# Late attention scores of a banded attention plus MLP kernel: plain float32 on quarters of the queries in place of high and low parts

## The chip, the cores and the metric

The kernel runs on one core of one Trainium2 chip. The metric is the device time of one execution in microseconds, the median of several runs. The core's engines work side by side and meet at semaphores: TensorE (PE: matmuls; PEld: its weight loads), VectorE (DVE), ScalarE (ACT), GpSimd (POOL) and SyncE (SP, which here issues nearly all DMA transfers). TensorE's instructions, SyncE's and GpSimd's run in the order in which the program is written; ScalarE's and VectorE's are put in order by a scheduler when the program is built.

## The reference, cut to what matters

Attention over 4 batches, 8 heads, 768 positions, head size 64. A query sees the first 8 positions and the 96 positions up to itself, with a bias that falls linearly with the distance (another slope for each head). Its result, all heads side by side, goes through an MLP with two weight matrices.

```python
scores = scale * np.matmul(q, k.transpose(0, 1, 3, 2))
is_global = pos[None, :] < int(n_global)                    # 8
is_local = (rel >= 0) & (rel < int(n_local))                # 96, rel = query - key
dist = np.where(is_global & ~is_local, float(n_local), np.abs(rel))
scores = np.where(is_global | is_local, scores - slopes[:, None, None] * dist, -1e9)
a = np.exp(scores - scores.max(-1, keepdims=True))
a = a / (a.sum(-1, keepdims=True) + 1e-09)
x = np.matmul(a, v)                     # then (batch * position, 512)
h = x @ w_in                            # 512 -> 2048
g = h * np.clip(h + 3.0, 0.0, 6.0) / 6.0
out = g @ w_out                         # 2048 -> 512
```

## The kernel before, in words

The 3072 tokens are 8 blocks of 384 tokens, each of three tiles of 128 queries. A block's attention is done in 4 pairs of heads, so there are 32 pairs, numbered 0 to 31. Each pair comes as one packed array (`pair_loads`): keys of both heads (head 0 on partitions 0 to 63, head 1 on 64 to 127; for each tile 96 earlier keys, 8 global ones and the tile's own 128, so 232 columns), the queries, and the values in two layouts.

Every product of the MLP is done three times with float32r parts, high times high, high times low, low times high. `first` (L168) has 12 matmuls for each of the 16 slices of the inner dimension, into a bank `hp`; `gate` (ACT L179, DVE L180), `high` (POOL L186 or ACT L188) and `rest` (DVE L193) make the parts of the activation; `second` (L200) has 9 matmuls of 512 columns into three banks `acc`. There are 8 x 16 slices in all.

The program has four stages:
- Up to about 66 us: the early pairs 0 to 8 (`plain` is true). Their scores (L857) are plain float32 matmuls of 64 rows; their exponentials are turned on TensorE (L904, L906, copied out by L908, `pt`). Beside it the weights are decoded from doubles (`decode`: L376, L388, L410 to L427).
- To about 158 us: the MLP of blocks 0 and 1, each slice as soon as its weights are decoded.
- To about 203 us (`rest_of_third`): the rest of block 1's MLP with pairs 9 to 11.
- Then the layers, blocks 2 to 7 (`twos`): one block's MLP with the next block's four pairs between its steps (`attention`). The last block has no attention beside it.

In the two last stages lists called `units` say what is written after which step of the MLP. In the layers a cycle of four units is: two `first` in a row, units 0 and 1, two `second` in a row, units 2 and 3. A pair takes six units: scores of a tile in each of the units 0, 1, 2; sums and norms of two tiles in 3; the third norm and the first `spread` in 4; the others and `fetch` in 5. Every second pair has the values of both pairs behind it, six units after its `fetch`.

A late pair, 9 to 31, has these steps:
- `split`: for each head ACT makes `q1`, the scaled query rounded to float32r (L831), POOL copies the keys to `kx` (L832), DVE makes the rest `q2` (L835) and the rest of the keys (L838). High and low part of a head's keys stand on the two halves of the partitions, and the queries come twice for that.
- `scores` (L861): for each tile and head two matmuls of 128 rows, 128 queries and 232 keys (128 in a block's first tile at a sequence's start). `bank` hands out one bank a tile, `sp` and `tp` in turn.
- `weigh`: DVE adds the distances and takes the minimum (L872), ACT makes the exponential and its sum (L876). `sum_up` (L886, L887) and `normalize` (POOL L896) divide by the sum.
- `spread`: DVE transposes blocks of 32 by 32 (L921), and a DMA writes them to DRAM (`there`, L923), one for each tile. `fetch` (L930): four DMAs bring them back turned, as `weights`.
- `values` (L948): 20 or 24 matmul instructions in 64 columns each, the two heads side by side.

## Time and profile before

| | |
|---|---|
| median of 3 runs | 660.93 us (660.62 to 661.12) |
| the profiled execution's own time | 660.32 us |
| its span, first to last instruction | 658.5 us |
| granted TensorE clock | 1.000 |
| late scores, L861 | 276 matmuls |
| fetches and writes of the exponentials | 92 and 69 DMAs |

A row of the profile reads: line, engine, operation, what is written <- what is read (shapes as partitions x elements), count | busy us, mean ns of one | idle time of the engine just before them, and what ended it. A row of the view in order of time begins with the start and the length in us, both from the span's start; equal neighbours are one row with a count, and the idle time before it stands in brackets with its releaser. Durations of neighbouring matmuls overlap, so the pace of TensorE is read from start to start. A plain float32 matmul of the code stands as two instructions in the trace.

### The profile page before, as it was taken

What the parts mean: (1) busy time and instruction counts of PE and PEld (TensorE: products, weight loads), DVE (VectorE), ACT (ScalarE), POOL (GpSimd) and SP (SyncE); (2) the same over time, 40 slices, a digit from 0 to 9 for tenths busy, and PEclk for the clock granted to TensorE, in tenths of its full rate; (3) what the DMA queues carried; (4) which work ended last, traced back from release to release, by engine and by line L of the source; (5) the groups of instructions that cost most, each with busy time, mean ns of one, the idle gap of its engine ahead of it and who ended that gap; (6) DMA issues with size and microseconds to landing.
All of it is one profiled execution on the core that took longest, in us unless ns stands there. A gap on an engine that the chain in (4) does not pass through costs nothing.

```text
span 658.5 us, 11444 instructions
## 1 busy us (share of the span) xinstructions
PE 647.1 (98%) x3933; PEld 581.0 (88%) x3933; DVE 423.2 (64%) x1147; ACT 286.4 (43%) x752; POOL 189.1 (29%) x377
## 2 busy tenths in 40 slices
PE   9989999999999999999999999999999999999997
PEld 7768899998989999999998999899899999989985
DVE  6888999998766876357654777356763676422222
ACT  6896877776333442244414333143331543121111
POOL 5663000002532433034241444124340342202100
PEclk9999999999999999999999999999999999999999
DMA  8676444432573675427552366615654275400001
GB/s 291 174 233 213 135 157 157 135 125 89 150 222 111 178 188 142 132 88 186 147 156 97 95 178 183 184 52 142 167 137 128 81 185 141 114 31 18 1 1 53
DMA packets 67316, 88.86 MB, mean 135 GB/s; under 512 B 10288, under 2 KB 52016, under 8 KB 67248
## 3 DMA queue, kind: packets, MB, share of 16 engines
q1 hardware_dynamic: 66960, 87.77, 45.9%
q8 instruction: 33, 0.54, 0.3%
q14 instruction: 35, 0.29, 0.1%
q10 hardware_dynamic: 288, 0.26, 0.1%
HBM read 65.08 MB, written 22.94 MB: 134 GB/s over the span
## 4 chain that ended last, share of the span: by engine, by line
PE 85%; DVE 9%; ACT 2%; issue 2%; POOL 1%; DMA 1%; POOLq 0%; DVEq 0%; ACTq 0%
PE hp L168 37%; PE acc L200 33%; PE xp L948 3%; PE sp L861 2%; PE tp L948 2%; PE tp L861 2%; PE sp L200 1%; DVE wz L423 1%; PE tp L200 1%; DVE wz L419 1%; PE xp L200 1%; DVE n L872 1%; ACT n L876 1%; DVE wz L411 1%; DVE g L180 1%
## 5 line engine op out<-in xcount | busy, mean ns | idle before, releaser
L179 ACT ACTIVATE g<-hp,small 128x384 f32<-128x384 f32 x127 | 73.6, 580 | 254.1 <-PE hp L168 147.2
L168 PE MATMUL hp<-xh,w1h 128*128 128x384 f32 x512 | 172.7, 337 | 0.4 <-ACT w1h L427 0.4
L168 PE MATMUL hp<-xh,w1l 128*128 128x384 f32 x512 | 172.3, 337 | 0.5 <-DVE w1l L416 0.5
L168 PE MATMUL hp<-xl,w1h 128*128 128x384 f32 x512 | 171.7, 335 | 0.0
L186 POOL TENSOR_SCALAR gh<-g 128x384 fp32r<-128x384 f32 x104 | 53.3, 512 | 289.1 <-DVE g L180 244.5
L180 DVE SCALAR_TENSOR_TENSOR g<-g,hp 128x384 f32<-128x384 f32 x128 | 70.2, 548 | 99.2 <-ACT g L179 98.8
L200 PE MATMUL acc<-w2h,gl 128*128 128x512 f32 x336 | 132.4, 394 | 0.2 <-DVE gl L193 0.2
L200 PE MATMUL acc<-w2h,gh 128*128 128x512 f32 x336 | 132.6, 395 | 0.0
L200 PE MATMUL acc<-w2l,gh 128*128 128x512 f32 x336 | 131.6, 392 | 0.0
L193 DVE TENSOR_TENSOR gl<-g,gh 128x384 fp32r<-128x384 f32 x128 | 75.9, 593 | 57.4 <-POOL gh L186 47.3
L896 POOL TENSOR_SCALAR n<-n,sums 128x232 f32<-128x232 f32 (+1 forms) x186 | 94.1, 522 | 48.4 <-DVE sums L887 42.5
L876 ACT ACTIVATE n<-n,least 128x232 f32<-128x232 f32 (+1 forms) x192 | 88.6, 464 | 30.4 <-DVE least L872 29.6
L168 PEld LDWEIGHTS hp<-xh,w1h 128*128 128x128 f32 x512 | 96.2, 188 | 3.4 <-ACT w1h L427 0.9
L168 PEld LDWEIGHTS hp<-xl,w1h 128*128 128x128 f32 x512 | 96.2, 188 | 2.1
L168 PEld LDWEIGHTS hp<-xh,w1l 128*128 128x128 f32 x512 | 96.0, 188 | 1.0 <-DVE w1l L416 0.8
L200 PEld LDWEIGHTS acc<-w2h,gl 128*128 128x128 f32 x336 | 63.0, 188 | 15.2 <-DVE gl L193 1.7
L200 PEld LDWEIGHTS acc<-w2h,gh 128*128 128x128 f32 x336 | 63.2, 188 | 13.3 <-issue 1.2
L200 PEld LDWEIGHTS acc<-w2l,gh 128*128 128x128 f32 x336 | 63.2, 188 | 11.6
L921 DVE STREAM_TRANSPOSE blocks<-n 128x256 f32<-128x256 f32 x127 | 49.4, 424 | 25.1 <-POOL n L896 23.1
L832 POOL TENSOR_SCALAR kx<-load 64x504 fp32r<-64x504 f32 (+1 forms) x46 | 29.1, 632 | 117.8 <-PE hp L168 96.1
L876 ACT ACTIVATION_READ_ACCUMULATOR n<-n,least 128x1 f32 x192 | 36.2, 188 | 0.0
L838 DVE TENSOR_TENSOR kx<-load,kx 64x504 fp32r<-64x504 f32 (+1 forms) x46 | 32.9, 715 | 1.8 <-POOL kx L832 0.4
(118 smaller groups left out, 731.5 us busy)
## 6 DMA issues: line engine op xcount, KB each, us to landing
wst<-w SPq DMA_DIRECT2D x32, 512.0 KB, 3.5
there<-blocks SPq DMA_DIRECT2D x58, 256.0 KB, 2.6
load<-pairs SPq DMA_DIRECT2D x23, 636.0 KB, 5.2
load<-pairs SPq DMA_DIRECT2D x32, 384.0 KB, 4.6
weights<-there SPq DMA_DIRECT2D x48, 192.0 KB, 3.6
weights<-there SPq DMA_DIRECT2D x44, 160.0 KB, 3.3
out<-o SPq DMA_DIRECT2D x23, 256.0 KB, 2.1
load<-pairs SPq DMA_DIRECT2D x8, 444.0 KB, 4.7
```

Of the source, the lines that this page charges most:

```text
L168: self.nc.tensor.matmul(hp, lhsT=self.w1(w, f)[:, kt, :], rhs=a[:, kt, :], start=(n == 0), stop=(n == 3 * NKT - 1))
L179: nc.scalar.activation(out=g, in_=hp, func=AF.Relu, bias=self.three, scale=1.0)
L180: nc.vector.scalar_tensor_tensor(out=g, in0=g, scalar=6.0, in1=hp, op0=ALU.min, op1=ALU.mult)
L186: self.nc.gpsimd.tensor_scalar(out=gh, in0=g, scalar1=1.0, scalar2=0.0, op0=ALU.mult, op1=ALU.add)
L193: self.nc.vector.tensor_tensor(out=gl, in0=g, in1=gh.bitcast(F32), op=ALU.subtract)
L200: self.nc.tensor.matmul(acc[tt], lhsT=a[:, tk], rhs=self.w2(w, f), start=(f == 0 and j == 0), stop=(f == NF - 1 and j == 2))
L832: nc.gpsimd.tensor_scalar(out=part["kx"][own, c], in0=k[own, c], scalar1=1.0, scalar2=0.0, op0=ALU.mult, op1=ALU.add)
L838: nc.vector.tensor_tensor(out=part["kx"][other, c], in0=k[own, c], in1=part["kx"][own, c].bitcast(F32), op=ALU.subtract)
L876: nc.scalar.activation(out=e[:, j, lo:W], in_=e[:, j, lo:W], func=AF.Exp, bias=self.least[:, i:i + 1], scale=-1.0, accum_out=self.sums[:, ...
L896: nc.gpsimd.tensor_scalar(out=e[:, j, lo:W], in0=e[:, j, lo:W], scalar1=over, scalar2=0.0, op0=ALU.mult, op1=ALU.add)
L921: nc.vector.transpose(out=blocks[:, :, s].rearrange("p b j q -> p j b q"), in_=e[:, :, c:c + P].rearrange("p j (b q) -> p j b q", b=4))
L948: nc.tensor.matmul(xps[j * D:(j + 1) * D, t * P:(t + 1) * P], lhsT=vt[0:K, t, j * D:(j + 1) * D], rhs=self.part(t, j, c, K), start=(c == 0 ...
```

## The change

For the late pairs the high and low parts go. The queries are scaled once a pair, in place, by ACT (`scale`, one operation of 128 x 384 with a scale for each partition from `over`), and the scores are plain float32 matmuls. A tile's 128 queries are split into four groups of 32. A group sees only 136 columns, its own window of 96 + 8 + 32 moved along by 32, in place of the tile's 232. Each of the 24 matmuls (3 tiles x 4 groups x 2 heads) uses a piece of the array of 64 rows by 32 columns. All are written together at the pair's first unit, head 0 into one bank, head 1 into another. Minimum, exponential and norm work on 136 columns.

A group's window begins 32 columns later than that of the group before. So in DRAM the blocks of group g go g places further, into a buffer whose unused places are set to zero once (`zeros_ahead`, 12 DMAs and a memset); two such buffers stay for good. The writes are four for each pair, one for each group, all behind the third tile's transposes; the fetches are eight. Every pair now fetches the whole of it. Masks for the groups (`packed_masks`) are made once by POOL, after the early pairs. The loads have the queries only once.

For one pair's scores on PE, pair 9 in the third block (`kx`, `q` are the parts, `load_72` is the loaded pair with its scaled queries; `acc` the banks of this stage), there stood:

```order
L861 MATMUL acc<-kx,q_1963 128x128
L861 MATMUL acc<-kx,q_1964 128x128
L861 MATMUL acc<-kx,q_1968 128x128
L861 MATMUL acc<-kx,q_1969 128x128
L861 MATMUL acc<-kx,q_1963 128x232
L861 MATMUL acc<-kx,q_1964 128x232
L861 MATMUL acc<-kx,q_1968 128x232
L861 MATMUL acc<-kx,q_1969 128x232
L861 MATMUL acc<-kx,q_1963 128x232
L861 MATMUL acc<-kx,q_1964 128x232
L861 MATMUL acc<-kx,q_1968 128x232
L861 MATMUL acc<-kx,q_1969 128x232
```

Now there stands, between the same neighbours (lines of the changed kernel: L206 is `second`, L174 `first`, L865 the packed scores):

```order
L206 MATMUL acc<-w2h_1028,gh 128x512
L206 MATMUL acc<-w2l_1029,gh 128x512
L206 MATMUL acc<-w2h_1028,gl 128x512
L865 MATMUL acc<-load_72 32x136 x24
L174 MATMUL hp<-xh,w1h_1026 128x384
L174 MATMUL hp<-xl,w1h_1026 128x384
```

The twelve are replaced by 24 smaller ones at the same place; in the layers the twelve stood in two groups, eight and four, on either side of a step of the MLP, and the 24 stand together.

On ACT, at the end of the early pairs (`pt` is a turned exponential on its way to the values, `wz` and `w1h` belong to the decoding, `gh` to the MLP), there stood:

```order
L908 COPY pt<-tp 128x2x128
L427 CAST w1h_143<-wz 128x4x128
L376 ACTIVATE wz<-wst 128x512
L188 CAST gh<-g 128x384
L908 COPY pt<-tp 128x512
L376 ACTIVATE wz<-wst 128x512
L154 CAST xh<-xp 128x384
```

Now:

```order
L930 COPY pt<-tp 128x2x128
L461 CAST w1h_143<-wz 128x4x128
L410 ACTIVATE wz<-wst 128x512
L194 CAST gh<-g 128x384
L851 ACTIVATE load_72<-load_72,over 128x384
L851 ACTIVATE load_73<-load_73,over 128x384
L930 COPY pt<-tp 128x512
L410 ACTIVATE wz<-wst 128x512
L160 CAST xh<-xp 128x384
```

The scalings of pairs 9 and 10 have moved ahead of the last copies of the early pairs; they wait for the pairs' loads and for `over`, which POOL writes. The old scalings of these pairs stood some 90 us later.

The diff, cut:

```diff
-QW = 2 * TB
+QW = TB
...
+GQ = 32
+GROUPS = P // GQ
+PW = PREV + NG + GQ
+SHIFT = GQ // 32
+AHEAD = 4 - SHIFT
+SPREAD = 4 + AHEAD
...
-                 "one": {"s": (o,), "x": (o,)}, "layers": {"s": (s, t), "t": (t,), "x": (x,)}}[self.stage][what]
+                 "one": {"s": (o,), "t": (o,), "x": (o,)}, "layers": {"s": (s,), "t": (t,), "x": (x,)}}[self.stage][what]
...
+    def packed_masks(self):
+        c, ts = self.const, self.nc.gpsimd.tensor_scalar
+        self.dl = c.tile([P, 2, PW], F32, name="dl")
+        self.over = c.tile([P, NPAIR], F32, name="over")
+        for h in range(H):
+            self.nc.gpsimd.memset(self.over[h % 2 * D:(h % 2 + 1) * D, h // 2:h // 2 + 1], float(-1.0 / (np.sqrt(D) * SLOPES[h])))
+        self.nc.gpsimd.memset(self.dl[:, 0], FAR)
+        for g in range(GROUPS):
+            rows, start = slice(g * GQ, (g + 1) * GQ), g * GQ
+            for out, d in ((self.dl[rows, 0, CB - start:], self.d0[rows, 0:start + GQ]),
+                           (self.dl[rows, 1], self.d1[rows, start:start + PW])):
+                ts(out=out, in0=d, scalar1=1.0, scalar2=0.0, op0=ALU.mult, op1=ALU.add)
...
-        for k in range(3):
-            pairs[0].split(k, False)
-        units[1] += [lambda: self.load_next(EARLY, False)]
+        pairs[0].scale()
...
-            at[0] += [lambda t=t, me=me: me.scores(t)() for t in range(NT)]
+            at[0] += [me.packed, lambda me=me: self.load_next(me.n, False)]
             at[1] += [me.sum_up] + [lambda t=t, me=me: me.normalize(t) for t in range(NT)]
-            at[2] += [lambda t=t, me=me: me.spread(t) for t in range(NT)] + [me.fetch]
-            for k in range(3):
-                at[k + 3 if last else k].append(lambda k=k, after=after: after.split(k))
+            at[2] += [lambda t=t, me=me: me.spread(t) for t in range(NT)] + [me.fetch, after.scale]
...
-            for t in range(NT):
-                at[t].append(lambda t=t, me=me: me.scores(t)())
-            if after:
-                at[3].append(lambda after=after: after.split(0))
+            at[0] += [me.packed, lambda me=me: self.load_next(me.n, False)]
             at[3] += [me.sum_up, lambda me=me: me.normalize(0), lambda me=me: me.normalize(1)]
             at[4] += [lambda me=me: me.normalize(2), lambda me=me: me.spread(0)]
             at[5] += [lambda me=me: me.spread(1), lambda me=me: me.spread(2), me.fetch]
-            for t in range(1, NT if after else 0):
-                at[t + 3].append(lambda t=t, after=after: after.split(t))
+            if after:
+                at[4].append(after.scale)
...
+    def scale(self):
+        nc, kk = self.nc, self.k
+        _, q, _, _ = kk.loaded(self.n)
+        nc.scalar.mul(out=q, in_=q, mul=kk.over[:, self.pr:self.pr + 1])
+
+    def packed(self):
+        nc, kk = self.nc, self.k
+        self.sums = kk.up.tile([P, 2, 2 * NT], F32, name="sums")
+        banks = [kk.bank(b)[:, 0:NT * PW].rearrange("p (t c) -> p t c", t=NT) for b in "st"]
+        keys, queries, _, _ = kk.loaded(self.n)
+        for t in range(NT):
+            for g in range(GROUPS):
+                own, c = slice(g * GQ, (g + 1) * GQ), t * TG + g * GQ
+                for j in range(2):
+                    rows = slice(j * D, (j + 1) * D)
+                    nc.tensor.matmul(banks[j][own, t], lhsT=queries[rows, t, own], rhs=keys[rows, c:c + PW], start=True, stop=True,
+                                     tile_position=(j * D, g * GQ))
+        for t in range(NT):
+            self.weigh(t, [bank[:, t] for bank in banks], kk.up.tile([P, 2, PW], F32, name="n"), 0)
...
-        nc.sync.dma_start(out=self.there[:, :, t, parts].rearrange("p b s c -> p b (s c)"),
-                          in_=blocks[:, :, parts].rearrange("p b s j q -> p b (s j q)"))
+        if t == NT - 1:
+            for g in range(GROUPS):
+                own = slice(g * GQ, (g + 1) * GQ)
+                nc.sync.dma_start(out=kk.there[self.n % 2][own, :, g * SHIFT:g * SHIFT + 4],
+                                  in_=self.blocks[own].rearrange("p s b t j q -> p s b (t j q)"))
...
-        for b in range(4):
-            self.nc.sync.dma_start(out=self.weights[32 * b:32 * b + 32].rearrange("p a t s j q -> p a (t s j q)")[:, :, part * 64:],
-                                   in_=self.there[:, b].rearrange("(a p) t s c -> p a (t s c)", a=4)[:, :, part * 64:])
+        for s in range(2):
+            for b in range(4):
+                rows = NG if s == 1 and b == 3 else 32
+                nc.sync.dma_start(out=to[32 * b:32 * b + rows, :, s],
+                                  in_=there[:, s, b + (0 if s else AHEAD)].rearrange("(a p) c -> p a c", a=4)[0:rows])
```

More of the change, by code (lines that the diff above doesn't have):

```diff
@@ L846, in scores @@
             self.sums = kk.up.tile([P, 2, 2 * NT], F32, name="sums")
-        if t != 1 or not self.plain:
-            self.banks = [kk.bank("s")[:, 0:2 * W].rearrange("p (i c) -> p i c", i=2) for _ in range(2 if self.plain else 1)]
-        sp = [self.banks[j][:, t % 2] if self.plain else self.banks[0][:, j] for j in range(2)]
+        if t != 1:
+            self.banks = [kk.bank("s")[:, 0:2 * W].rearrange("p (i c) -> p i c", i=2) for _ in range(2)]
+        sp = [self.banks[j][:, t % 2] for j in range(2)]
         e = kk.up.tile([P, 2, W], F32, name="n")
@@ L870, in weigh @@
             else:
-                d, scale = (kk.d0 if lo else kk.d1), SLOPES[h]
-            nc.vector.tensor_tensor_reduce(out=e[:, j, lo:W], in0=sp[j][:, lo:W], in1=d, op0=ALU.add, op1=ALU.min, scale=scale,
+                d, scale = kk.dl[:, 0 if self.first(t) else 1], SLOPES[h]
+            nc.vector.tensor_tensor_reduce(out=e[:, j, lo:end], in0=sp[j][:, lo:end], in1=d, op0=ALU.add, op1=ALU.min, scale=scale,
                                            scalar=3.0e38, accum_out=self.least[:, i:i + 1])
@@ L875, in weigh @@
             i = 2 * t + j
-            nc.scalar.activation(out=e[:, j, lo:W], in_=e[:, j, lo:W], func=AF.Exp, bias=self.least[:, i:i + 1], scale=-1.0,
+            nc.scalar.activation(out=e[:, j, lo:end], in_=e[:, j, lo:end], func=AF.Exp, bias=self.least[:, i:i + 1], scale=-1.0,
                                  accum_out=self.sums[:, 0, i:i + 1])
@@ L889, in normalize @@
     def normalize(self, t):
-        nc, e, lo = self.nc, self.rows[t], self.low(t)
+        nc, e, lo, end = self.nc, self.rows[t], self.low(t), self.end
         for j in range(2):
@@ L936, in part @@
             return self.pts[t][0:K, j, c, :]
[L937 removed]
+        return self.weights[0:K, :, c, t, j]
     def values(self, bank="x"):
@@ L943, in values @@
         for t in range(NT):
-            two = not self.low(t)
+            two = not self.first(t)
             for c in range(2 if two else 1):
```

92 lines of the change are left out of this document (37 added, 55 removed).

## The prediction

> **What bounds the kernel now.** I read the busy shares first, then the busy time by stretches, then the order in time around the steps that the change replaces. The head of the page:
>
> ```profile
> span 658.5 us, 11444 instructions
> PE 647.1 (98%) x3933; PEld 581.0 (88%) x3933; DVE 423.2 (64%) x1147; ACT 286.4 (43%) x752; POOL 189.1 (29%) x377
> ```
>
> The stretch from 238 us to the end of the layers, in the view by windows (columns: stretch, length, then busy us and instructions of PE, PEld, DVE, ACT, POOL, granted clock, DMA share, GB/s):
>
> ```profile
> 238.00:653.00 415.00, 415.00 (x2478) 377.04 (x2475) 224.92 (x601) 130.48 (x359) 120.06 (x236) 1.00 0.42 114
> ```
>
> PE has work in all 415.00 of 415 us, at the full clock. So what shortens PE's stream there shortens the kernel one for one, and what VectorE, ScalarE or GpSimd save brings nothing by itself. It matters only where PE waits for them. Before 152 us that happens: the decoding of the weights holds PE back at two places (used below).
>
> **The scores on PE.** The late pairs (9 to 31, 23 of them) use 12 matmuls each; all of them in one row of the windows view, and one pair in time:
>
> ```profile
> 150.00:653.00 503.00, 37.77 (x276) 37.08 (x276) 1.00 0.44 122
> 213.18 0.40 PE L200 MATMUL acc<-w2h,gl 128*128 128x512 f32 x1
> 213.41 0.60 PE L861 MATMUL tp<-kx,q 128*128 128x232 f32 x4
> 213.85 0.61 PE L861 MATMUL sp<-kx,q 128*128 128x232 f32 x4
> 214.30 0.34 PE L168 MATMUL hp<-xh,w1h 128*128 128x384 f32 x1
> ```
>
> 276 = 23 x 12. Durations overlap, so I count from start to start: 8 matmuls take 214.30 - 213.41 = 0.89 us, 0.111 each, and 12 take 1.33 us. Entering and leaving costs nothing visible.
>
> The new pair has 24 plain float32 matmuls of 64 rows by 32 columns on 136 keys: 8 places in the array, three rounds. The trace shows what plain float32 costs in the early scores, which run two halves of the rows at once, 232 keys wide:
>
> ```profile
> 25.06 0.46 PE L857 MATMUL sp<-load 64*128 64x232 f32 x1
> 25.07 0.46 PE L857 MATMUL acc<-load 64*128 64x232 f32 x1
> 25.36 0.36 PE L857 MATMUL sp<-load 64*128 64x232 f32 x1
> ...
> 25.56 0.36 PE L857 MATMUL sp<-load 64*128 64x232 f32 x1
> ```
>
> Each matmul of the code is two instructions here (one pair has 6 in the code, 12 in the trace), so the new pair has 48. Both halves start within 0.01 us, and the second instruction of one half doesn't hold up the first of the other. A step of both takes 25.56 - 25.36 = 0.20 us, 0.86 ns a key. If all eight places overlap as these two do, a step for 136 keys takes 0.117 us and a pair needs 3 x 2 = 6 steps, 0.70 us. The overhead of such a stay I take from the values, which also put two matmuls side by side:
>
> ```profile
> 314.57 0.34 PE L168 MATMUL hp<-xh,w1l 128*128 128x384 f32 x1
> 314.84 1.32 PE L948 MATMUL xp<-weights,load 128*64 128x128 f32 x20
> 315.99 1.27 PE L948 MATMUL tp<-weights,load 128*64 128x128 f32 x20
> 317.19 0.50 PE L200 MATMUL acc<-w2h,gh 128*128 128x512 f32 x1
> 317.52 0.40 PE L200 MATMUL acc<-w2l,gh 128*128 128x512 f32 x1
> ```
>
> From 314.57 to 317.52 are 2.95 us. Two ordinary steps (0.17 and 0.23) and 20 steps of 128 x 0.86 ns (2.20) leave 0.35 us for changing into and out of the split array. Eight starts in turn, up to 0.01 us apart, add some 0.05. So a pair takes 0.70 + 0.35 + 0.05 = 1.10 us against 1.33: -0.23 us, x 23 = **-5.3 us**. Bounds: 1.00 us (the turns hidden and the overhead a little less; -7.6) and 1.25 us (0.15 more, if PE's queue is refilled late; -1.8). 1.10 is nearest to the rows.
>
> Here a page speaks against the change. The Trainium skill ("TensorE: Matmul & The Clock Gate", section "Wait — 56ns, not 53.3ns?") says that matmul starts never come closer than about 25 ns, however few columns they have. By it 48 instructions would take 1.20 us, as an estimate from that page, and a pair 1.55 with the overhead: +5.1 us for 23 pairs in place of -5.3. The rows above show two starts 0.01 us apart, but on average no stay is denser than the values' 1.15 us for 20, so no row here settles it. By rows alone the case stands among the rivals.
>
> **One wait goes.** Pair 12 has its third query tile wait for a bank:
>
> ```profile
> 204.54 0.71 PE L861 MATMUL sp<-kx,q 128*128 128x232 f32 x4 [0.38 <-DVE least L872]
> ```
>
> PE is idle for 0.38 us. Now all three tiles of a head share one bank, so nothing in a pair waits for a bank: **-0.4 us**. No other wait of that kind stands on PE after 213 us.
>
> **Two scalings are early, on ScalarE.** `scale` for pairs 9 and 10 now stands among the last early pairs, ahead of a copy that PE waits for. The old scaling, and that place:
>
> ```profile
> L831 ACT ACTIVATE q<-load 128x384 fp32r<-128x384 f32 x46 | 21.5, 517 | 25.2 <-issue 9.2 <-PE sp L861 6.4 <-PE acc L861 5.1
> 57.99 0.58 ACT L908 COPY pt<-tp 128x512 f32<-128x512 f32 x1
> 58.72 0.30 PE L904 MATMUL tp<-ident,n 128*128 128x128 f32 x1 [0.33 <-ACT pt L908]
> 149.86 0.44 PE L168 MATMUL hp<-xh,w1h 128*128 128x384 f32 x1 [0.44 <-ACT w1h L427]
> 150.95 0.44 PE L168 MATMUL hp<-xh,w1l 128*128 128x384 f32 x1 [0.47 <-DVE w1l L416]
> ```
>
> Two scalings of 0.5 us ahead of the copy move PE's step at 58.72 by 1.0 us. Queued behind them on ScalarE is also the decoding's next `wz`, so VectorE comes late too. At 149.86 and 150.95 PE waits 0.91 us for the decoding anyway; a late PE would simply wait less there, as far as the decoding isn't late as well. Between 0 and 2.0 us (if GpSimd's eight small memsets that the scalings wait for, and its masks beside VectorE, cost once more as much); I take **+0.8 us**. The masks have no row of their own; GpSimd has nothing else from 57 to 150 us.
>
> **The way of the weights becomes longer.** The exponentials go to DRAM and come back: three writes and four fetches a pair, now four writes, all behind the third tile's transposes, and eight fetches. The second pair of each two has little time. Pair 15 (norms, writes, fetches, use):
>
> ```profile
> 252.48 1.31 POOL L832 TENSOR_SCALAR kx<-load 64x400 fp32r<-64x400 f32 x2
> 253.89 3.14 POOL L896 TENSOR_SCALAR n<-n,sums 128x232 f32<-128x232 f32 x6
> 256.12 2.25 SPq L923 DMA_DIRECT2D there<-blocks  x3
> 261.91 1.92 SPq L930 DMA_DIRECT2D weights<-there  x4
> DMA to landing us min/median/max: 2.9/3.7/3.9
> 267.60 1.53 PE L948 MATMUL tp<-weights,load 128*64 128x128 f32 x24
> ```
>
> The last fetch is issued at about 263.5 and lands by 267.4, 0.2 us ahead of its use. Now: the copy of the keys is gone from ahead of the norms (-1.4 us, 253.89 - 252.48), and the norms are shorter. A row with two norms of 128 and two of 232 columns gives their length:
>
> ```profile
> 287.12 1.59 POOL L896 TENSOR_SCALAR n<-n,sums 128x128 f32<-128x128 f32 x4 [3.04 <-DVE sums L887]
> ```
>
> At about 0.36 each for 136 columns, six take 2.2 instead of 3.14 (-0.9). Three more writes behind the last transpose at the fetches' spacing of 0.48 us: +1.4. Four more fetches: +1.9. The last one moves half the bytes and lands perhaps 1.3 us sooner (2.6 instead of 3.9, as the writes of 256 KB):
>
> ```profile
> there<-blocks SPq DMA_DIRECT2D x58, 256.0 KB, 2.6
> ```
>
> The sum is -0.3: no wait, for 15 and for the like pairs with more room. Pair 11, in the third block, has no key copy ahead of its norms:
>
> ```profile
> 185.14 2.86 POOL L896 TENSOR_SCALAR n<-n,sums 128x128 f32<-128x128 f32 x6
> 192.23 1.76 SPq L930 DMA_DIRECT2D weights<-there x4
> DMA to landing us min/median/max: 2.7/3.2/3.7
> 197.60 1.32 PE L948 MATMUL acc<-weights,load 128*64 128x128 f32 x20
> ```
>
> It lands at about 197.3 (193.6 + 3.7). Norms -0.7, writes +1.4, fetches +1.9, landing -1.1: +1.5, less 0.3 of room: PE waits **+1.2 us** once; between 0 (short issues) and 2.3 (landing as now).
>
> At nothing I cost what VectorE (two q2, two kx, narrower minima), ScalarE and GpSimd save, and the smaller loads: PE's work covers all of it. The load of the next-but-one pair now waits on SyncE for the packed matmuls; behind it stand only writes that come some 8 us later, and the scaling that needs it comes a whole pair later.
>
> **Sum** against the profiled execution's 660.32 us (span 658.5): -5.3 - 0.4 + 0.8 + 1.2 = -3.7, 656.6. The runs' median lies 0.6 above that execution, so 657.2.
>
> **Rivals.**
> Fewer than eight places at once (15%). Reading four column groups, or starting so many matmuls, may not go at the pace of two; the trace never shows more than two side by side. The point of balance: the six steps may take 0.98 us (1.33 - 0.35) instead of 0.70, so with under six of eight at a time the pair is slower than before. Four at a time: 12 x 0.117 + 0.35 = 1.75 us, +9.7 us instead of -5.3: 672.2. Two at a time, as now: 24 steps, 3.16 us: 704.6. Against it: the two halves start 0.01 us apart and don't hold each other up. The 25 ns of the Trainium skill ("TensorE: Matmul & The Clock Gate") would give 667.6 by the same sum.
>
> The weights come late for all second pairs (9%). If the norms start no earlier (the sums then decide) and a fetch lands as slowly as now, the second pair is 1.4 + 1.9 - 0.9 = 2.4 us later than before. Pair 15 has 0.2 us of room, and pair 25 has the most:
>
> ```profile
> 462.31 1.73 SPq L930 DMA_DIRECT2D weights<-there  x4
> weights<-there SPq DMA_DIRECT2D x44, 160.0 KB, 3.3
> 470.71 1.27 PE L948 MATMUL tp<-weights,load 128*64 128x128 f32 x20
> ```
>
> (The last fetch is issued at 463.6 and lands by 466.9 to 467.2, some 3.5 us ahead.) With the ten second pairs of the layers spread between 0.2 and 3.5, those under 2.4, some seven, wait 1.1 on average, 7 us in all, and pair 11 waits 1 us more: 665.2.
>
> The packed pair takes as long as the old one (10%): overhead of 0.55 us with eight places. Then 4.4 of the 5.3 are gone: 661.6.
>
> **Chances.** The forecast has 66%; its own range, with the bounds above but not all of them at once on one side, is 653 to 661.5. The third rival lies inside 662.5, the second around 665; a range of 653 to 664.5 leaves out the first, half of the second and a little at the low end, 20%. About 0.2% (1.3 us, so 659.6 to 662.3 for the median now) is what a measurement can tell from no change. Faster: 0.60 of the forecast's 0.66 and 0.01 of the third rival, 0.61. Same: 0.06 + 0.08 + 0.02 (forecast, third, second), 0.16. Slower: 0.15 + 0.07 + 0.01 (first, second, third), 0.23.
>
> **What would show it.** Right: from the last layer matmul to the first one after a packed stay about 1.1 us beyond an ordinary step, with eight starts close together; PE still without gaps after 240 us; no wait ahead of the third tile at pair 12; PE's step near 58.7 about a microsecond later; a gap of about 1 us ahead of pair 11's values near 197. Wrong: steps well over 0.117 us in the packed stay, or values of the second pairs with gaps ahead of them.

## The result and the profile after

The changed kernel takes 677.02 us (median of 4 runs, 675.32 to 682.26) against 660.79 us before: 1.0258 times as long (95% interval 1.020 to 1.0317), where 657.2 was forecast, with 653.0 to 664.5 as its range. The profiled execution took 675.99 us, 15.7 more than the one of before.

The head of the page, with the row of the granted clock in 40 slices, then the stretch from 238 us to the end of the layers (columns as before: busy us and instructions of PE, PEld, DVE, ACT, POOL, clock, DMA share, GB/s):

```profile
span 674.2 us, 13085 instructions
PE 648.5 (96%) x4761; PEld 570.2 (85%) x4761; DVE 356.3 (53%) x1066; ACT 267.3 (40%) x729; POOL 153.8 (23%) x349
...
PEclk9999999999998998999999999899999999999999
```

```profile
238.00:668.00 430.00, 420.02 (x3121) 372.27 (x3120) 178.66 (x555) 118.46 (x353) 91.46 (x205) 0.99 0.39 108
```

Two things are new: PE stands idle for 10 of these 430 us, and the clock isn't full in all slices. The engines that were to be relieved are (VectorE is busy for 356 us, in place of 423), and that brings nothing, as forecast.

One packed stay, its last layer step before and the first ones behind:

```profile
303.04 0.39 PE L206 MATMUL acc<-w2h,gl 128*128 128x512 f32 x1
303.36 0.30 PE L865 MATMUL sp<-load 64*32 64x136 f32 x1
...
303.41 0.30 PE L865 MATMUL tp<-load 64*32 64x136 f32 x1
303.50 0.28 PE L865 MATMUL sp<-load 64*32 64x136 f32 x1
...
303.62 0.28 PE L865 MATMUL sp<-load 64*32 64x136 f32 x1
...
304.05 0.28 PE L865 MATMUL tp<-load 64*32 64x136 f32 x1
304.25 0.45 PE L174 MATMUL hp<-xh,w1h 128*128 128x384 f32 x1
304.54 0.34 PE L174 MATMUL hp<-xl,w1h 128*128 128x384 f32 x1
```

Eight starts lie within 0.05 us (303.36 to 303.41), and the next eight follow 0.14 and then 0.12 us later. From 303.04 to 304.54 are 1.50 us; less two ordinary steps (0.23 and 0.17) the stay costs 1.10 us, the number of the forecast; 18 of the 23 stays, read in this way, take 1.10. So the loss lies elsewhere. What PE waited for:

```profile
PE sp L865 <- DVE xl L161: 4.3, 3, 3.3
PE acc L974 <- DMA weights<-there: 3.5, 2, 2.6
PE sp L974 <- DMA weights<-there: 3.3, 5, 1.3
...
PE hp L174 <- DVE g L186: 2.3, 1, 2.3
```

(us in total, times, longest.) The wait of 3.3 us for `xl`, ahead of pair 15's scores, is the longest. Followed back over the engines, two rows each of SyncE, ScalarE and PE in the view in order of time:

```profile
237.35 3.53 SPq L956 DMA_DIRECT2D weights<-there  x8
240.99 3.63 SPq L327 DMA_DIRECT2D load<-pairs  x3
245.01 0.62 ACT L851 ACTIVATE load<-load,over 128x384 f32<-128x384 f32 x1 [5.13 <-DMA load<-pairs]
248.53 0.47 ACT L160 CAST xh<-xp 128x384 fp32r<-128x384 f32 x1
248.17 0.39 PE L206 MATMUL acc<-w2h,gl 128*128 128x512 f32 x1
251.91 0.43 PE L865 MATMUL sp<-load 64*32 64x136 f32 x1 [3.35 <-DVE xl L161]
```

ScalarE sits for 5.13 us in front of a scaling (L851) whose load has only been issued at 240.99 us, behind the fetches of pair 13. It is the scaling of pair 16, whose scores come at 290 us. Behind it on ScalarE stand the gates of the layers and the halves `xh` of pair 12's and 13's output; `xl` needs `xh`, the bank of pair 13's values needs `xl`, and the packed matmuls of pair 15 need that bank. (That the chain runs over these steps is read from the order in time and from what each step waited for; the first experiment tests its cause.) All scalings of the kernel in one view:

```profile
L851 ACT ACTIVATE load<-load,over x23: 601/616/620, 58.6 to 553.0; 128x384 f32<-128x384 f32 x23
its engine sat idle before it (us, times) until:
  DMA load<-pairs: 88.8, 19
```

19 of 23 wait for their load, 88.8 us in all; the row of the old scalings, in the prediction, names no load among the causes of their 25.2 us. And behind a long stall PE runs slowly:

```profile
250.00:254.00 4.00, 2.10 (x50) 1.69 (x51) 2.07 (x7) 0.05 (x1) 0.60 (x2) 0.66 0.33 73
254.00:258.00 4.00, 4.00 (x14) 4.00 (x13) 1.37 (x12) 2.71 (x13) 0.00 (x0) 0.50 0.53 138
258.00:262.00 4.00, 4.00 (x21) 3.61 (x21) 1.11 (x2) 0.28 (x1) 0.52 (x1) 0.99 0.73 190
```

The granted clock (third column from the right) is 0.50 for some 7 us; 14 instructions in 4 us stand in the second row where the third has 21. The trace has three such stretches before the last layer matmul: 200.1 to 206.9, 251.3 to 258.1 and 425.4 to 428.8 us.

Where the 15.7 us went can be read by setting the start of each layer matmul beside that of the same matmul before (both kernels have the same 2688, in the same order; the figure is how far the changed kernel lies behind):

| up to (time of before) | what lies there | change, us |
|---|---|---|
| 157.8 | early pairs, decoding | 0.0 |
| 192.6 | packed stays of pairs 9 to 11 | -0.7 |
| 201.2 | pair 11's values late (4.5), half clock behind them (1.9) | +6.4 |
| 232.7 | pairs 12 to 14, the wait at pair 12 gone | -1.4 |
| 247.5 | pair 15's scores late (4.2), half clock behind them (2.2) | +6.4 |
| 269.1 | pair 15's values late | +1.5 |
| 387.4 | pairs 16 to 22 | -1.6 |
| 413.3 | pair 23's scores and a gate late (3.0), half clock behind them (1.6) | +4.6 |
| 423.8 | pair 23's values late | +2.0 |
| 559.0 | pairs 24 to 31 | -1.7 |

Before rounding the changes add up to 15.6 us. The clock is in two of the other figures too: the half clock began within pair 11's values and ahead of pair 15's scores. From the first packed matmul of pair 15 to the next layer matmul are 1.54 us, where the stay at 303.36 has 0.89; the second half of pair 11's values took 1.48 us from its start to the next layer matmul, where all of them took 1.24 before.

### The profile page after: what moved, and what is told of

It reads as the page before. It is cut to its first block, busy times and chain, and to the rows that moved or that the text cites. A ratio compares the mean times of both kernels' runs of the same rounds, so it can differ in the third digit from the quotient of the medians.

```text
span 674.2 us, 13085 instructions
## 1 busy us (share of the span) xinstructions
PE 648.5 (96%) x4761; PEld 570.2 (85%) x4761; DVE 356.3 (53%) x1066; ACT 267.3 (40%) x729; POOL 153.8 (23%) x349
## 4 chain that ended last, share of the span: by engine, by line
PE 63%; DMA 10%; DVE 8%; SPq 6%; ACT 5%; POOL 4%; issue 3%; POOLq 0%; ACTq 0%
PE hp L174 28%; PE acc L206 25%; DMA there<-blocks 4%; SPq L956 4%; DMA load<-pairs 3%; ACT n L898 2%; POOL n L918 2%; DVE blocks L940 2%; SPq L945 2%; PE xp L974 2%; ACT g L185 2%; DVE g L186 2%; DMA weights<-there 1%; PE sp L865 1%; PE sp L206 1%
## 5 line engine op out<-in xcount | busy, mean ns | idle before, releaser
L174 PE MATMUL hp<-xh,w1h 128*128 128x384 f32 x512 | 176.2, 344 | 2.3 <-DVE g L186 2.3
L174 PE MATMUL hp<-xh,w1l 128*128 128x384 f32 x512 | 174.2, 340 | 0.1
L174 PE MATMUL hp<-xl,w1h 128*128 128x384 f32 x512 | 173.6, 339 | 0.0
L206 PE MATMUL acc<-w2h,gh 128*128 128x512 f32 x336 | 133.5, 397 | 0.0
L206 PE MATMUL acc<-w2h,gl 128*128 128x512 f32 x336 | 132.1, 393 | 0.2 <-DVE gl L199 0.2
L206 PE MATMUL acc<-w2l,gh 128*128 128x512 f32 x336 | 131.9, 393 | 0.0
L199 DVE TENSOR_TENSOR gl<-g,gh 128x384 fp32r<-128x384 f32 x128 | 71.6, 559 | 66.2 <-POOL gh L192 57.4
L174 PEld LDWEIGHTS hp<-xh,w1h 128*128 128x128 f32 x512 | 97.6, 191 | 8.9 <-issue 3.5
L898 ACT ACTIVATE n<-n,least 128x136 f32<-128x136 f32 (+2 forms) x192 | 79.4, 415 | 55.3 <-DVE least L894 54.5
L174 PEld LDWEIGHTS hp<-xl,w1h 128*128 128x128 f32 x512 | 97.8, 191 | 2.6
L174 PEld LDWEIGHTS hp<-xh,w1l 128*128 128x128 f32 x512 | 97.6, 191 | 0.8 <-DVE w1l L450 0.7
L918 POOL TENSOR_SCALAR n<-n,sums 128x136 f32<-128x136 f32 (+2 forms) x186 | 82.2, 460 | 40.9 <-DVE sums L909 30.8
L206 PEld LDWEIGHTS acc<-w2h,gh 128*128 128x128 f32 x336 | 63.4, 189 | 15.3 <-issue 3.6
L206 PEld LDWEIGHTS acc<-w2h,gl 128*128 128x128 f32 x336 | 63.2, 188 | 14.4 <-DVE gl L199 0.9
L206 PEld LDWEIGHTS acc<-w2l,gh 128*128 128x128 f32 x336 | 63.3, 188 | 11.5
L940 DVE STREAM_TRANSPOSE blocks<-n 128x256 f32<-128x256 f32 x138 | 51.2, 424 | 23.0 <-POOL n L918 20.5
L851 ACT ACTIVATE load<-load,over 128x384 f32<-128x384 f32 x23 | 14.1, 615 | 88.8 <-DMA load<-pairs 88.8
L865 PE MATMUL sp<-load 64*32 64x136 f32 x480 | 19.6, 289 | 4.3 <-DVE xl L161 4.3
```

What stands on the lines that cost most here:

```text
L174: self.nc.tensor.matmul(hp, lhsT=self.w1(w, f)[:, kt, :], rhs=a[:, kt, :], start=(n == 0), stop=(n == 3 * NKT - 1))
L199: self.nc.vector.tensor_tensor(out=gl, in0=g, in1=gh.bitcast(F32), op=ALU.subtract)
L206: self.nc.tensor.matmul(acc[tt], lhsT=a[:, tk], rhs=self.w2(w, f), start=(f == 0 and j == 0), stop=(f == NF - 1 and j == 2))
L851: nc.scalar.mul(out=q, in_=q, mul=kk.over[:, self.pr:self.pr + 1])
L865: nc.tensor.matmul(banks[j][own, t], lhsT=queries[rows, t, own], rhs=keys[rows, c:c + PW], start=True, stop=True, tile_position=(j * D, g ...
L898: nc.scalar.activation(out=e[:, j, lo:end], in_=e[:, j, lo:end], func=AF.Exp, bias=self.least[:, i:i + 1], scale=-1.0, accum_out=self.sums ...
```

## The experiments

Two theories stood after the trace. Theory 1: the scaling on ScalarE waits for its load and holds up the gates, the exponentials and the halves of x behind it. Theory 2: the way of the weights (turn, write, fetch) has become too long, because nothing is written until the last transposes are done.

**Scalings as written.** ScalarE's order is the scheduler's, while those of PE, SyncE and GpSimd are held to the written order. The edit holds the scalings of pairs 11 to 31 too:

```diff
+        before = [i.name for i in nc.cur_bb.bb.instructions if i.engine == mybir.EngineType.Activation and "Tile" not in type(i).__name__][-1]
         nc.scalar.mul(out=q, in_=q, mul=kk.over[:, self.pr:self.pr + 1])
+        if self.n > EARLY + 1: kk.tc.add_manual_dep(nc.cur_bb.bb.instructions[-1], before, mybir.DependencyInfo(
+            mybir.DependencyClass.NoSync, mybir.DependencyReason.DATA), reason="as written")
```

> The changed kernel, with one edit: ScalarE keeps the scalings of pairs 11 to 31 behind the instruction of ScalarE that is written last ahead of them, so that the scheduler can't draw them forward to a place where their load hasn't landed. Theory 1 (the scaling: ScalarE waits for the load, and the gates, exponentials and parts of x behind it come late): ScalarE's 88.8 us of waiting for loads go to under 10; the waits of PE ahead of pair 15's scores (3.35 us), at 409 and at 424 us go with the two drops of the granted clock behind them (5 us in all), pair 11's values wait about 1.6 us in place of 3.5 and so keep the full clock: 655 to 660 us. Theory 2 (the weights' way alone: four writes behind the last transposes): ScalarE waits for other things in place of the loads, the stalls stay, 673 to 679 us.

Measured: 660.61 us, 0.9998 times the kernel before (0.9988 to 1.0008), so 16.4 us less than the changed kernel, just above the range of theory 1. ScalarE waits for no load any more; the scaling of pair 16 now stands behind the gate and runs at once:

```profile
241.66 0.58 ACT L185 ACTIVATE g<-hp,small 128x384 f32<-128x384 f32 x1 [1.96 <-DVE gl L199]
242.14 0.60 ACT L851 ACTIVATE load<-load,over 128x384 f32<-128x384 f32 x1
242.68 0.48 ACT L160 CAST xh<-xp 128x384 fp32r<-128x384 f32 x1
```

No wait of PE is left between 210 and 650 us; the late values of pairs 15 and 23 went with the late scores. One part missed: pair 11's values wait as long as before.

```profile
PE acc L974 <- DMA weights<-there: 3.7, 2, 2.5
```

Its sums came 3.0 us sooner (182.0 in place of 185.0 us), its last weights only 0.3 us. So for 15 to 31 theory 1 holds, for 11 it doesn't.

**Two writes.** The four writes of 32 partitions become two of 128, to the same addresses (cut: the buffer gets a second view, `turned`, whose rows lie a group apart):

```diff
-            for g in range(GROUPS):
-                own = slice(g * GQ, (g + 1) * GQ)
-                nc.sync.dma_start(out=kk.there[self.n % 2][own, :, g * SHIFT:g * SHIFT + 4],
-                                  in_=self.blocks[own].rearrange("p s b t j q -> p s b (t j q)"))
+            for s in range(2):
+                k = s * SPREAD * NT * 64
+                nc.sync.dma_start(out=kk.turned[self.n % 2][:, :, k:k + 4 * NT * 64],
+                                  in_=self.blocks[:, s].rearrange("p b t j q -> p (b t j q)"))
```

> The changed kernel, with one edit: the exponentials of a pair go to DRAM in two writes of 128 partitions in place of four of 32 partitions, to the same addresses. Both theories: the last write is issued 1.3 us sooner, and fetches, loads and scalings follow by 1.0 to 1.9 us. Theory 2 (the weights' way): nearly all stalls are 0.1 to 2.7 us long, so most of them go: 659 to 664 us. Theory 1 (the scaling): the waits of ScalarE for loads grow shorter by as much, but stay (over 50 us of the 88.8), PE still waits ahead of pair 15's scores for 1.5 to 2.5 us: 666 to 671 us.

Measured: 822.56 us, 1.2457 times the kernel before; both theories missed by 150 us. SyncE's order shows where:

```profile
184.72 1.13 SPq L946 DMA_DIRECT2D there<-blocks  x2
197.01 3.54 SPq L957 DMA_DIRECT2D weights<-there  x8
```

The fetches wait for the writes until 197.01, 11.7 us behind the last issue. For the 23 pairs this time is 11.1 to 12.2 us; with four writes, in the changed kernel, it was 3.1 to 4.6 us. In the trace 16 completions belong to each write of four, and only 5 to each of these two. The first of the 5 comes 0.9 to 1.0 us behind the issue, the other four between 6.8 and 11.6 us behind it. The target of the new write has the four groups as its outermost dimension. The Trainium skill ("DMA: Bandwidth & Descriptors", section "Why a DMA increments its semaphore by 16 and not by 1") says that a transfer uses as many of the 16 engines as divide the slowest dimension of both sides, and that the engines not used are counted at once; by it these writes ran on four engines (four completions and one jump), and the trace agrees. The run says nothing on the theories.

**Both edits.**

> Both edits: the scalings of pairs 11 to 31 stay where they are written, and two writes in place of four. Theory 1 and theory 2 agree that no stall over 0.5 us is left on PE behind 160 us, and that the clock stays full: the packed pairs' saving shows whole, 23 x 0.25 = 5.8 us, so 654 to 656 us. A rival with a cause not seen so far (the packed matmuls themselves lower the clock): the drops stay, over 660 us.

Measured: 785.39 us (1.1894; 1.1855 to 1.1933). The two writes spoil this run too; that it lies 37 us below the run with them alone shows only that the scalings cost something there as well.

**The writes alone, in the kernel before.** Its own scores, scalings and fetches, but four late writes (and with them, as in the changed kernel, one buffer for the transposed blocks in place of three; the trace shows no wait for it):

```diff
-        self.bp = self.pool("bp", 3, side="right")
+        self.bp = self.pool("bp", 1, side="right")
...
-        blocks = kk.bp.tile([P, 4, 2, 2, 32], F32, name="blocks")
+            self.blocks = kk.bp.tile([P, 4, NT, 2, 2, 32], F32, name="blocks")
...
-        nc.sync.dma_start(out=self.there[:, :, t, parts].rearrange("p b s c -> p b (s c)"),
-                          in_=blocks[:, :, parts].rearrange("p b s j q -> p b (s j q)"))
+        for g in range(4 if t == NT - 1 else 0):
+            own, part = slice(g * 32, (g + 1) * 32), slice(64 if self.low(0) else 0, None)
+            nc.sync.dma_start(out=self.there[own].rearrange("p b t s c -> p b (t s c)")[:, :, part],
+                              in_=self.blocks[own].rearrange("p b t s j q -> p b (t s j q)")[:, :, part])
```

> The kernel before, with one edit: its exponentials go to DRAM as in the changed kernel, in four writes of 32 partitions behind the third tile's transposes, in place of one write behind each tile's; scores, loads and fetches are its own. Theory 2 (the writes make the way 3.4 us longer by themselves): with the room that the second pairs had (0.2 to 3.5 us) they wait 1.5 us on average, 17 us in all and more if the clock drops: 672 to 682 us. If the writes cost 1.5 us only, as the prediction's sum had it, five pairs wait 3.3 us in all: 663 to 665 us. Theory 1 alone (the stalls need the scaling): within 2 us of the kernel before.

Measured: 670.57 us (1.0137; 1.0109 to 1.0166), 9.9 us more than the kernel before. That is in none of the ranges: below the 672 to 682 of theory 2, above the 663 to 665 by the prediction's price of the writes, and far from theory 1 alone.

```profile
PE tp L950 <- DMA weights<-there: 3.8, 4, 1.4
PE acc L950 <- DMA weights<-there: 2.6, 1, 2.6
```

The values of second pairs now wait (L950 is the values' line). So late writes cost by themselves. With the scalings as written, the changed kernel has the same late writes, and only pair 11 waits for them. What pays the price back for the others is most likely that the copies of the keys are gone from ahead of the norms and that the norms are shorter (pair 11 had no such copies); no run separates these.

**Pair 11: another queue for its writes.** In the scalings-as-written kernel, SyncE around pair 11:

```profile
184.31 3.54 SPq L956 DMA_DIRECT2D weights<-there  x8
187.96 0.82 SPq L327 DMA_DIRECT2D load<-pairs  x2
188.87 3.55 SPq L945 DMA_DIRECT2D there<-blocks  x4
195.10 3.55 SPq L956 DMA_DIRECT2D weights<-there  x8
```

Pair 11's last transpose ended at 186.8, but its writes stand behind pair 10's fetches and two loads. Theory 3: that queue makes them late.

```diff
-                nc.sync.dma_start(out=kk.there[self.n % 2][own, :, g * SHIFT:g * SHIFT + 4],
+                (nc.gpsimd if self.n < 12 else nc.sync).dma_start(out=kk.there[self.n % 2][own, :, g * SHIFT:g * SHIFT + 4],
```

> The first experiment's kernel (scalings of pairs 11 to 31 as written), with one more edit: the writes of pairs 9, 10 and 11 are issued by GpSimd in place of SyncE. Theory 3 (SyncE's queue is the bound of the third block's pairs: a pair takes 1.9 us of write issues, 4.0 us until the last of them lands, 3.2 us of fetch issues and 0.4 to 0.9 us for loads, about 10 us, against 9.5 us from pair to pair, so that pair 11's writes are issued 2.0 us behind its transposes): the writes of pair 11 start within 0.5 us of its last transpose, its last fetch lands some 2 us sooner, near 196.5 us, its values wait under 1.2 us in place of 3.7, the clock stays full, and the span shortens by 4.5 to 6 us: 654.5 to 656 us. Rival (a write's own 4 us from issue to landing make pair 11 late, not the queue): its last fetch lands at most 0.5 us sooner, the stall and the drop of the clock stay: 659.5 to 661 us.

Measured: 661.31 us (0.9996; 0.998 to 1.0012). The writes did follow their transposes at once (188.3, then 188.6 us), yet they took up to 6.1 us to land (2.9 to 6.1, median 4.0), and the next fetches began later than before:

```profile
DMA to landing us min/median/max: 2.9/4.0/6.1
```

```profile
196.50 3.55 SPq L956 DMA_DIRECT2D weights<-there  x8
```

The loads, issued at 189.19 and 189.65 beside them, landed among them (194.2 and 195.9; the last write 196.4). The place in SyncE's queue alone wasn't it. The run is no clean test of it, though: GpSimd, which now issues writes between its other work, came later to its copies and norms, so that pair 11's transposes ended 1.5 us later (188.3 in place of 186.8), and PE waited 0.7 us for a copy at 173 us.

**All writes from GpSimd.** `nc.gpsimd` for all pairs.

> As the run before, but GpSimd issues the writes of all pairs. Theory 3: nothing more is gained in the layers, where no value waits any more; SyncE's queue gets shorter by 1.9 us a pair. If a write costs GpSimd as much as SyncE (0.63 us of issue each, and the wait for the transposes ahead of it, some 3.4 us a pair) the copies gh behind them come up to 1 us late at places, which PE does not see: 654.5 to 656.5 us. If GpSimd needs more than 1.5 us for one write, gh is late and PE waits: over 660 us.

Measured: 661.88 us (1.001; 0.9998 to 1.0021). GpSimd needs 0.5 us for a write, far less than the 1.5 us from which a loss was expected; still nothing is gained, and the values of one more pair wait (0.9 us near 502 us).

**Idle matmuls while PE waits.** Twelve matmuls ahead of pair 11's values, into the bank that they overwrite:

```diff
-        xps = kk.bank(bank)[:, 0:TB]
-        for t in range(NT):
+        xps, any_ = kk.bank(bank)[:, 0:TB], kk.three.broadcast_to([P, P])
+        for t in [None] * (12 * (self.n == 11)) + list(range(NT)):
+            if t is None: nc.tensor.matmul(xps[:, 0:P], lhsT=any_, rhs=any_, start=True, stop=True); continue
```

> The first experiment's kernel, with 12 idle matmuls of 128 columns (into the bank that the values then overwrite) ahead of pair 11's values, so that PE is busy while it waits for the weights. If the drop of the granted clock behind this stall (200.0 to 206.9 us, 1.95 us of the drift against the kernel before) comes from PE standing idle, the clock stays full and only the wait is left: 658.5 to 659 us. If it has another cause (the packed matmuls, the kernel's power), it stays: 660.6 us, or more by what the idle matmuls delay.

Measured: 659.63 us (0.9976; 0.9962 to 0.9989). The first two rows are the stretch around pair 11's values with the scalings as written alone, the last two the same stretch with idle matmuls (PE busy, clock, DMA share, GB/s):

```profile
200.00:204.00 4.00, 3.17 (x17) 0.51 0.94 300
204.00:208.00 4.00, 4.00 (x17) 0.64 0.26 88
```

```profile
200.00:204.00 4.00, 2.95 (x33) 1.00 0.80 192
204.00:208.00 4.00, 4.00 (x24) 1.00 0.81 311
```

The clock stays full with the weights as late, the same packed matmuls and the same data: it is the idle PE that lowers it. The time lies above the 658.5 to 659 us expected. In the profiled execution the clock dropped elsewhere, near 60 us, where PE waits for the early pairs' copies (0.82 between 58 and 62 us); the 12 runs lie between 658.2 and 661.7 us.

**All scalings as written**, those of pairs 9 and 10 too (the condition on `self.n` left out).

> The first experiment's kernel, with the scalings of pairs 9 and 10 left where they are written too, so that none stands among the early pairs. PE's step near 59 us should come 1.0 us sooner. Theory (the decoding of the weights covers it, as the 0 end of the prediction's term had it): the two waits for the decoding near 150 us take the 1.0 us back, and the time is within 0.5 us of the first experiment's 660.6. The prediction's middle value: 0.8 us less, 659.8 us.

Measured: 661.01 us (0.9994; 0.9984 to 1.0005), as the first experiment. PE's step near 59 us comes sooner (59.38 in place of 60.06), and the waits for the decoding near 150 us are back: the early scalings cost nothing on average, the 0 end of the term.

**Two loads out of the way.** The load of pair 11's values ahead of pair 10's fetches, that of pair 13's keys behind pair 11's:

```diff
-            at[0] += [me.packed, lambda me=me: self.load_next(me.n, False)]
+            at[0] += [me.packed]
...
-            at[2] += [lambda t=t, me=me: me.spread(t) for t in range(NT)] + [me.fetch, after.scale]
-        units[10].append(lambda: pairs[0].values("x"))
+            at[2] += [lambda t=t, me=me: me.spread(t) for t in range(NT)] + ([] if p == 1 else [me.fetch]) + [after.scale]
+            at[2 if p == 2 else 0].append(lambda me=me: self.load_next(me.n, False))
+        units[10] += [lambda: pairs[0].values("x"), pairs[1].fetch]
```

> The first experiment's kernel, with SyncE's order changed in the third block alone: the load of pair 11's values stands ahead of pair 10's fetches in place of behind them, and the load of pair 13's keys and queries behind pair 11's fetches in place of ahead of its writes. In the first experiment these two loads (187.96 and 188.41 us) were issued between pair 10's fetches and pair 11's writes, and the first of the writes landed only behind them (192.26). Theory 3 in its second form (what is queued ahead of pair 11's writes, on SyncE and at the DMA engines, makes them late): the writes are issued at about 187.6 and have landed by 192 in place of 195.0, the last fetch lands by 198 in place of 200.7, PE waits about 1.9 us in place of 3.7, and the clock stays full: 656.5 to 657.5 us. If a write needs its 4.2 us anyway: the last fetch lands at about 199.5, the clock drops as before: 659 to 660 us.

Measured: 658.22 us (0.9957; 0.9944 to 0.9971).

```profile
188.86 2.49 SPq L946 DMA_DIRECT2D there<-blocks  x4
194.11 3.53 SPq L957 DMA_DIRECT2D weights<-there  x8
```

The writes are issued as before (188.86), since pair 10's fetches began 0.9 us later, but they have landed 1.0 us sooner (194.11 in place of 195.10). PE waits 2.4 us in place of 3.7, and the low clock lasts half as long (3.41 us in place of 6.83). The time lies between the two ranges. So the second form of theory 3 holds in part. What is left is the way itself: 5.2 us from first write to first fetch, and 5.5 to the last weights, together more than the 9.5 us from pair to pair.

**The same with six idle matmuls.**

> As the run before, with 6 idle matmuls ahead of pair 11's values. If the wait there is short enough for the clock to stay full by itself, they bring nothing (656.5 to 657.5 us, as the run before); if the clock drops in the run before, they take the drop away and it is 1.5 to 2 us faster than that run.

Measured: 657.26 us (0.9942; 0.9928 to 0.9955); the intervals of this and the run before overlap. In its profile the clock is full around 200 us and again dropped near 60 us (0.95 between 58 and 62).

**A third room for the loads**, with the scheduler's scalings of the changed kernel:

```diff
-        return self.room[(n if n < EARLY else LAST[(n - EARLY) % ROOMS]) % MORE]
+        return self.room[n % MORE] if n < EARLY else self.late[(n - EARLY) % 3]
...
-            self.load(n + ROOMS, values)
+            self.load(n + 3, values)
```

> The changed kernel, with ScalarE's order left as it is there (the scalings drawn forward), but with three rooms for the loads of the late pairs in place of two, so that a load is issued a whole pair earlier. Theory 1 (the loads come too late for the place of the scalings): ScalarE's waits for loads go from 88.8 us to under 15, the waits of PE at pairs 15 and 23 go as in the first experiment, only pair 11's stay: 659 to 662 us. If the place of the scalings hurts in another way (their 0.6 us ahead of gates and exponentials): over 668 us.

Measured: 680.43 us (1.0309; 1.0288 to 1.033): a clear miss.

```profile
L855 ACT ACTIVATE load<-load,over x23: 598/616/624, 58.7 to 532.6; 128x384 f32<-128x384 f32 x23
...
  DMA load<-pairs: 85.2, 17
```

The loads come a pair earlier, and ScalarE still waits 85.2 us for them. From pair 15 on a scaling starts 16 to 46 us ahead of its pair's matmuls in the changed kernel, 37 to 60 us here, and 3 to 26 us where it stays as written. It seems that the scheduler moves the scaling forward as far as it takes the load to allow, so that more room moves the wait and doesn't end it; what the scheduler assumes of a load is in no run. The expectation had taken the order of ScalarE for unchanged. The scalings do stand at like places (245.01 us there and 246.70 us here, each ahead of a gate), but each is that of the next pair (17 in place of 16).

**All together**: every scaling as written, the loads aside, six idle matmuls.

> All scalings as written (those of pairs 9 and 10 too), SyncE's two loads aside in the third block, and 6 idle matmuls ahead of pair 11's values: the three edits that took something away, in one kernel. The profile of the run before this one (with the scalings of pairs 9 and 10 still early) had left the early pairs with PE 2.6 us behind the kernel before, 1.6 us of it by a drop of the clock near 60 us. If the early scalings bring that drop, it is gone here, and of the 23 x 0.25 = 5.8 us of the packed pairs and the 0.4 of pair 12 only the rest of pair 11's wait is lost, about 2 us: 656 to 657 us, ratio to the kernel before 0.993 to 0.995. If the drop near 60 us has another cause, it comes in some of the runs here too: a median of 657 to 658 us with a spread of 2 us.

Measured: 656.40 us, 0.993 times the kernel before (0.9916 to 0.9944), 4.9 us less.

```profile
span 654.5 us, 13114 instructions
PE 641.0 (98%) x4773; PEld 565.3 (86%) x4773; DVE 357.7 (55%) x1066; ACT 268.4 (41%) x729; POOL 153.5 (23%) x349
```

```profile
PE acc L976 <- DMA weights<-there: 1.0, 1, 1.0
```

That is within the 656 to 657 us expected. One wait of 1.0 us for weights is left, and the clock doesn't drop before the last layer matmul (its mean over the span is 0.999). A saving of the forecast's size (3.7 us) is there, but the change alone doesn't bring it: it needed three more edits, of which the forecast knew nothing.

## Why the prediction was wrong

**The packed stay (-5.3): right.** 1.10 us forecast, 1.10 measured, 0.12 us a step with all eight places at work. Where nothing waits, the comparison gives 0.27 us a pair in place of 0.23, so the old pairs took a little more than the 1.33 us counted. The first rival, fewer places at once, is out: 48 starts lie within 0.69 us (303.36 to 304.05), 15 ns apart on average. The 25 ns between starts that the Trainium skill gives ("TensorE: Matmul & The Clock Gate", section "Wait — 56ns, not 53.3ns?") is not a bound for matmuls in different places of the array: the trace disagrees.

**Pair 12's wait (-0.4): right.** About 0.6 us, the part of its step in the comparison (0.9) that is not the 0.27 us of its stay.

**The early scalings (+0.8): too much.** PE's step came 1.66 us late at that place,

```profile
60.38 0.30 PE L926 MATMUL tp<-ident,n 128*128 128x128 f32 x1 [1.58 <-ACT pt L930]
```

and by 157.8 us nothing of it was left: the waits at 149.86 and 150.95 took it in, as the lower end said. With all scalings held back the step was still 0.7 us late, so 1.0 us of the 1.66 belongs to the scalings, as forecast; what delays the rest no run separates. What the term lacked is that the longer wait sometimes lowers the clock there.

**What was costed at nothing: the step that failed.** The prediction said of the load of the next-but-one pair that behind it stand only writes that come 8 us later, "and the scaling that needs it comes a whole pair later". The second half failed: it took the place in the code for the place on the engine. The section on the change shows that two scalings stand some 90 us ahead of the old ones, and the prediction priced these two; it didn't ask where the other 21 stand. 19 of the 23 waited for their load, 88.8 us in all, with gates, exponentials and parts of x behind them. And the load's own place was overlooked: it is issued behind the fetches of the pair before, which wait for writes to land. Pair 14's packed matmuls ended at 232.9 us; the load that they set free was issued at 240.99. Holding the scalings back gave 16.4 us, more than the whole loss against the kernel before.

**Pair 11 (+1.2, at most 2.3): mis-sized, 6.4.** The rows of SyncE, two from before and two from after:

```profile
186.77 2.58 SPq L923 DMA_DIRECT2D there<-blocks  x3
192.23 1.76 SPq L930 DMA_DIRECT2D weights<-there  x4
189.84 3.48 SPq L945 DMA_DIRECT2D there<-blocks  x4
195.70 3.56 SPq L956 DMA_DIRECT2D weights<-there  x8
```

From the last transpose (189.8) to the first fetch are 5.9 us where 3.4 were before (188.8 to 192.23): +2.5 in place of the +1.4 for writes. The sum had priced the issues of three more writes; but all of a pair's data, too, now starts on its way behind the transposes. The fetches, +1.9 less 1.1, cost 0.2 (5.1 us before and 5.3 now from first issue to last landing): the later issues land sooner. The norms save 0.3, not 0.7 (2.57 us in place of 2.86: a norm takes the 0.36 us counted, but the first of the six 0.77). They began 1.3 us later, behind a wait of ScalarE of 4.97 us for a load ahead of the exponentials. That is 3.7; with the start due 0.7 us sooner by the packed stays, less 0.3 of room, 4.1 of the 4.5 us seen. PE stood idle for 3.5 of these (the row of the waits above); most of the rest is the half clock on the second half of the values. The other 1.9 us is the half clock behind them.

**The clock: in no term and no rival.** Behind the stalls half clock took 5.7 of the 15.7 us (1.9 + 2.2 + 1.6), and some more within pair 11's values and pair 15's scores. It always began in a stall that other causes made, or up to 1.2 us behind it.

**The second rival (weights late for all second pairs, 665.2)** came nearest to a part of what happened: in the kernel before the late writes alone cost 9.9 us. In the changed kernel with the scalings as written only pair 11 waits for its weights by more than 0.2 us, so all second pairs waiting is not what made the loss. The range failed because the place of the scalings had no price at either end.

## What to carry to other kernels

Where a scheduler orders an engine, a new instruction need not stand where it was written: look at that engine's order for every copy of it, and ask for each what it waits for and who stands behind it. A stall's price on PE is its length and the half clock behind it: here waits of 2.3 to 3.4 us cost another 1.6 to 2.9 us by the half clock, one of 1.3 us nothing more. Data that is written early, piece by piece, hides its own transfer behind the work on the next piece; gathered into one write behind the last piece, all of it is on the path.

## What the runs showed of the hardware

The clock drops on a grid: every low stretch in the 14 traces begins a whole number of 3.41 us behind the first entry of the clock's record, and lasts a whole number of them too, if the record doesn't end first: one or two in most traces, up to five (17.07 us) in the two runs with two writes. The Trainium skill ("TensorE: Matmul & The Clock Gate", section "What's actually happening") gives that window, and one idle window as the condition. The length agrees; the condition doesn't, if idle means all of it: the drop at 425.4 us followed an idle stretch of only 2.3 us,

```profile
424.21 0.44 PE L174 MATMUL hp<-xh,w1h 128*128 128x384 f32 x1 [2.32 <-DVE g L186]
```

in a window (421.96 to 425.37) of which PE had worked a third. A window with 1.3 us of waiting (at 280 us; PE busy for 0.62 of it) brought none. Counted over all 14 traces, what tells the two apart is the share of the window in which PE was busy: it lay between 0 and 0.49 in each of the 57 windows at full clock ahead of a drop (the idle ends of the executions among them), and at 0.48 or more in each that no drop followed. So the border was near half a window. (The profile models the ends of matmuls, so the shares are rough.) The record begins at another place in each execution, 4.0 to 10.4 us into the span, so where the windows fall on a stall differs: the stall near 60 us left PE busy for 0.47 and 0.49 of a window in the two profiles with a drop there, for 0.48 to 0.81 in the other eight with the two early scalings.

Eight small matmuls side by side kept the pace of two: a step of 136 columns took 0.12 us, 0.86 ns a column, as the steps of the early scores in the prediction. Two writes whose target has four as its outermost size took about three times as long, from the last issue to the first fetch, as four writes of the same bytes (11.1 to 12.2 us in place of 3.1 to 4.6).
